# A hand-written instruction list, written anew: chunked state-space scan and squared-ReLU feed-forward on one Trainium2 core

## The chip, the cores and the metric

The kernel runs on one core of a Trainium2 chip. The metric is the device time of one launch in microseconds (us). An execution under the profiler gives a trace, and from it a profile: which engine did what, when, and what released it. The engines are TensorE (PE, its weight loads PEld), VectorE (DVE), ScalarE (ACT), GpSimd (POOL) and SyncE (SP), which here only issues transfers. Each runs its own instructions in order, and they wait for one another by semaphores.

## The reference

A state-space scan over 4 batches, 8 heads and 768 positions in chunks of 32, and on its output a feed-forward layer with a squared ReLU:

```python
cum = np.cumsum(la, axis=-1)                       # la: log of the clipped a
L = np.exp(cum[:, :, :, None] - cum[:, :, None, :]) * causal
M = np.einsum('bhin,bhjn->bhij', Cc, Bc) * L
y[:, :, sl] = M @ xc + (Cc @ state) * np.exp(cum)[..., None]
state = decay_full * state + sum(Bc * xc * decay_from_j)
...
h = np.maximum(x @ w_in, 0.0)                      # x: y as 3072 x 256
return h * h @ w_out                               # w_in 256 x 2048, w_out 2048 x 256
```

Inputs and output are float32.

## The kernel before

**Units.** The work is cut into 12 units (L86): unit k is batch k % 4 and the third k // 4 of the positions, 256 positions of all 8 heads. Unit k's output T[k] is block k of the feed-forward layer. A block has eight steps: a first product, `mm1` (L398, written a0 to a7 for block 0, b0 to b7 for block 1, and so on), a ReLU on ACT into `hb` (L410), a square on DVE (L413, written qa0 and so on), and a second product, `mm2` (L424, A0 to A7). Step 7 of a block ends with its store.

**Preparing a unit.** The running products P of a come from a clamp (`clamp`, ac0 and ac1), a scan on DVE (`scan`, sk0 and sk1) and a small product on TensorE (`prep_p`). ac0, sk0 and `first_p` (sp) make P0 for the first third (units 0 to 3), from the loads fa0 and fa1; ac1, sk1 and `second_p` (p) make the rest, from la0 to la3. C is multiplied by P (`prep_c`, pc), B is copied (`prep_b`, pb), both into the tile jt of the unit; x is multiplied by 1/P (`prep_x`, px). For units 0 to 3 jt is transposed on TensorE (`ph_tr`, tr, with trC and trB for unit 0) and copied out of PSUM (`ph_trc`, tc); from unit 4 on by a DMA of SP. Then come the scores (`ph_mt`, mt, four PSUM banks). A score is masked straight from PSUM by DVE (`ph_mask`, mk) or first copied by ACT (`ph_score`, sc) and then masked by DVE or POOL (`ph_mask_sb`, ms). `ph_u` (u) adds the unit's part to the state, `ph_intra` (ina, inb: two masks each) and `ph_carry` (ca) build the output in two banks, and `ph_t` (t) copies it to T. For the first four units the state goes through `ph_sd_first` (sf, DVE, from PSUM) and `ph_uc` (us, ACT, from PSUM); ph_z and ph_sd (za, zb, sa, sb) carry it on.

**The order.** `ORDER` (L48 to L70) is a list of such tokens, written out by hand. The function `one` (L667) issues them one after the other, and that is the order of each engine's own queue. A letter behind a colon names the engine (v DVE, a ACT, p POOL, s SP); pc, pb and px without one are on POOL. wi0 to wi3 and wo0 to wo3 are the quarters of w_in and w_out, issued by POOL with a cast to bf16 (L137, L142). id12:128 issues 12 products of 128 columns that nobody reads (`idle`, L474). gB3 (`gate`, L130) is a small POOL write to the tile that the load of unit 3's B fills, so this load, and those behind it in SP's queue, wait for POOL.

**Banks.** PSUM has eight banks, and two engines that use one bank are kept apart by semaphores even where they use other columns of it. Banks are given out in turn (`bank`, `pair`, L354 and L360) as the list is read. Unit 0's output is in banks 6 and 7, and its u writes columns 256 to 319 of the same two (L259 to L268). So sf and us read banks that the intra products write.

Of the kernel before, what the change touches and what calls it, by code (L numbers as in the profile page):

```python
# [30 lines left out]
def kernel(  # L31
# [16 lines left out]
    ORDER = """  # L48
        fa1:a jz0:v ef jz1:p id12:128 ti fa0:s la0:s id15:128 pi eb ldB0:s ac0:v ldC0:a sk0 ku sp la1:a pbh0:p hd
        id1:256 pc0:v pbl0:v mb:a id7:128 trC0 ps iv:8:16 tcC0:1:a tcC0:0:v trB0 la2:s tcB0:2:v pk id4:128 iv1:0:8  # L50
        id2:256 ldx0:s mt0 wi0 la3:s px0:v ldC1:s ac1:p su id8:128 ldB1:s wi1 ldx1:s u0:67 mk0 mk0 mk0 pc1:p sc0
        pb1:a tr1 to id5:256 tc1:1:a tc1:0:v jz2:a ms0:p sk1 fq sf0 wo0 wi2 px1:p mt1 ina0 inb0 ca0 mk1 mk1 t0:aa
        sc1 us0 pp1:a mk1 a0 ldC2:s a1 u1 ina1 ms1:v pc2 inb1 p2 sf1 ca1 t1:va us1 a3 qa1 ldB2:s qa0 wo1 wi3 a2
        wo2 b0 qa3 qb0 b1 qb1 fr b2 b3 A0 A1 B0 pb2:p B1 tr2 zb0 qb3 b4 a4 iv:32:64 zb1 tc2:1:v qa2 tc2:0:v b5 sb1
        sb0 qb4 ldx2:s a5 qb2 qa4 mt2 gB3 sc2 ldB3:s ldC3:s B3 iv:16:32 px2 mk2 sc2 A3 ms2:v A2 mk2 qa5 a6 b6
        ms2:p B2 a7 qb5 pb3:a qa6 b7 A5 u2 ina2 ldx3:s inb2 sf2 wo3 pc3 px3 ld4 A4 tr3 ca2 tc3:1:v t2:aa B4 us2 B5
        tc3:0:v u3:45 pc4 mt3 us3 sc3 c5 qb7 qb6 mk3 za3 pb4 ld5 c3 qa7 c4 qc5 c0 tr4 qc3 px4 pb5 sa3 c1 c6 ld6
        qc4 pc5 tr5 qc0 A6 px5 pq A7 wm c2 B6 c7 C0 ms3:v mk3 qc6 mk3 qc7 afC2 pc6 pb6 B7 C3 C6 C4 qc1 bk rg4 C1
        qc2 d1 d0 za4 sa4 mk4 mk4 d3 mk4 C5 d4 qd0 d2 mk4 px6 C2 C7 ld7 zb4 qd1 sb4 qd2 qd3 zb3 rg5 sb3 D0 tr6 mk5
        za5 zb5 sa5 sb5 D1 iv:64:96 mk5 d5 qd4 D2 pb7 d6 qd5 d7 qd6 D3 zb2 e0 qd7 mk5 e1 qe0 sb2 D4 mk5 D5 ld8 pc7  # L60
        e2 qe1 D6 e3 qe2 px7 D7 rg6 e4 qe3 za6 sa6 tr7 zb6 mk6 e5 qe4 sb6 e6 qe5 e7 qe6 mk6 E0 E1 E2 E3 ld9 px8
        mk6 f0 qe7 E4 f1 qf0 pc8 E5 pb8 E6 mk6 f2 qf1 f3 qf2 E7 rg7 mk7 F0 f4 qf3 za7 tr8 F1 F2 f5 qf4 f6 qf5 f7
        qf6 g0 qf7 zb7 sa7 sb7 mk7 F3 mk7 F4 pc9 pb9 px9 ld10 g1 qg0 F5 mk7 g2 qg1 F6 g3 qg2 F7 rg8 za8 zb8 sa8
        sb8 g4 qg3 G0 mk8 tr9 g5 qg4 G1 mk8 g6 qg5 G2 g7 qg6 G3 mk8 h0 qg7 G4 pc10 pb10 px10 ld11 h1 qh0 G5 mk8 h2
        qh1 G6 h3 qh2 G7 rg9 za9 zb9 sa9 sb9 h4 qh3 H0 mk9 tr10 h5 qh4 H1 mk9 h6 qh5 H2 h7 qh6 H3 mk9 i0 qh7 H4
        pc11 pb11 px11 i1 qi0 H5 mk9 i2 qi1 H6 i3 qi2 H7 rg10 za10 zb10 sa10 sb10 i4 qi3 I0 mk10 tr11 i5 qi4 I1
        mk10 i6 qi5 I2 i7 qi6 I3 mk10 j0 qi7 I4 j1 qj0 I5 mk10 j2 qj1 I6 j3 qj2 I7 rg11 za11 zb11 sa11 sb11 j4 qj3
        J0 mk11 j5 qj4 J1 mk11 j6 qj5 J2 j7 qj6 J3 mk11 k0 qj7 J4 k1 qk0 J5 mk11 k2 qk1 J6 k3 qk2 J7 rg12 k4 qk3
        K0 k5 qk4 K1 k6 qk5 K2 k7 qk6 K3 l0 qk7 K4 l1 ql0 K5 l2 ql1 K6 l3 ql2 K7 l4 ql3 L0 l5 ql4 L1 l6 ql5 L2 l7
        ql6 L3 ql7"""  # L70
# [172 lines left out]
    def mm(begun, i, quads, dst, w, v, pos):  # L243
        need = [(i, q) for q in quads if (i, q) not in begun]
        begun.update(need)
        assert len(need) in (0, len(quads))
        nc.tensor.matmul(dst, w, v, start=bool(need), stop=False, skip_group_check=True,  # L247
                         **({} if pos is None else {"tile_position": pos}))
# [92 lines left out]
    def ph_sd_first(k):  # L341

        v, b = live[k], UNITS[k][0]
        S_d = spool.tile([128, 256], BF16, tag=f"Sd{b}0", name=f"Sd{k}_0")
        nc.vector.tensor_tensor(  # L345
            out=_fap(S_d, 0, [[128, 2], [32, 4], [1, 32]]),
            in0=_fap(pp, v["h"][0] * 512 + 256, [[32, 2], [0, 4], [1, 32]]),
            in1=_fap(Pquad, 4 * total(0, b, 0), [[0, 2], [1, 4], [0, 32]]), op=ALU.mult)
# [108 lines left out]

    with tc.manual_schedule():
# [78 lines left out]
        def clamp(m, eng):  # L537
            eng.tensor_scalar(out=a_cl[m], in0=a_nat[m], scalar1=1e-6, scalar2=1.0, op0=ALU.max, op1=ALU.min)  # L538
# [237 lines left out]
```

## Time and profile before

| | |
|---|---|
| runs | 117.34, 117.55, 115.72 us (median 117.34) |
| the profiled execution | 116.09 us |
| its span, first to last instruction | 114.4 us |
| mean granted TensorE clock | 0.985 |
| bytes read from and written to HBM | 10.58 MB, 3.15 MB |

The span is cut into 40 slices in the page; a digit is a share in tenths. A row of a stage has its start and end, its length, busy us and instructions of each engine, and at the end the granted clock, the DMA share and GB/s. A row of the chain has a start, a length, and the engine and line that the end of the program depended on at that time. A row of the timeline has a start, a length, engine, line, operation, what is written and read, and how many; in brackets stands how long the engine had been idle before, and what released it.

### The profile page before, as it was taken

The numbers are of one execution on the slowest core, as the hardware profiler recorded it, in microseconds if no ns is written. First come the engines' busy times: TensorE is split into PE (matmuls) and PEld (weight loads), VectorE is DVE, ScalarE is ACT, GpSimd is POOL, SyncE is SP. The second block draws the span as 40 slices with busy tenths as digits, with TensorE's granted clock in tenths as the row PEclk, the third lists the DMA queues.
The fourth block names the chain that finished last, engine by engine and source line by source line (L and its number), as shares of the span: only waits on it lengthen the run. The fifth ranks groups of instructions, "written<-read, shape, count | busy, mean of one in ns | idle before, by whom it ended". The sixth has DMA issues, their size and how long they took to land.

```text
span 114.4 us, 4062 instructions
## 1 busy us (share of the span) xinstructions
PE 108.4 (95%) x1658; PEld 96.5 (84%) x1658; DVE 84.4 (74%) x185; ACT 77.4 (68%) x158; POOL 52.2 (46%) x98
## 2 busy tenths in 40 slices
PE   7967899999999999999999999999999999999990
PEld 7845499898898889989989989989889899899980
DVE  2697566998899799989965989659578388345430
ACT  1744777677794785686587687786777776966840
POOL 7699950499298946659402769047020020000000
PEclk9999599999999999999999999999999999999999
DMA  2999999099998908988628538350051020020202
GB/s 40 198 196 193 217 196 188 10 183 169 189 163 140 317 10 181 215 192 164 131 80 158 112 113 149 87 145 19 6 141 22 6 95 0 14 83 0 92 6 92
DMA packets 47827, 13.47 MB, mean 118 GB/s; under 512 B 44288, under 2 KB 45888, under 8 KB 47808
## 3 DMA queue, kind: packets, MB, share of 16 engines
q1 hardware_dynamic: 44864, 10.88, 45.9%
q0 software_dynamic: 1664, 2.10, 11.4%
q10 hardware_dynamic: 1280, 0.23, 1.0%
q8 instruction: 13, 0.21, 0.7%
q14 instruction: 6, 0.05, 0.1%
HBM read 10.58 MB, written 3.15 MB: 120 GB/s over the span
## 4 chain that ended last, share of the span: by engine, by line
PE 87%; POOL 3%; DMA 3%; SPq 2%; issue 1%; ACT 1%; DVE 0%; ACTq 0%
PE pp L405 38%; PE pp L432 37%; PE pp L247 7%; PE pp L222 3%; DMA a_nat<-in_a_dram 3%; POOL mts L240 1%; SPq L565 1%; SPq L126 1%; POOL jt L159 1%; POOL w_in_b L140 1%; PE pp L197 1%; ACT T L210 1%; DVE Sd L345 0%; POOL a_cl L538 0%; SPq L116 0%
## 5 line engine op out<-in xcount | busy, mean ns | idle before, releaser
L410 ACT ACTIVATE hb<-pp 128x512 bf16<-128x512 f32 x96 | 54.6, 603 | 22.5 <-PE pp L405 21.4
L416 DVE TENSOR_TENSOR h<-hb 128x512 bf16<-128x512 bf16 x96 | 46.0, 498 | 12.1 <-ACT hb L410 11.8
L405 PE MATMUL pp<-T,w_in_b 128*128 128x256 bf16 x384 | 54.2, 276 | 0.5 <-ACT T L210 0.5
L432 PE MATMUL pp<-w_out_b,h 128*128 128x256 bf16 (+1 forms) x400 | 53.8, 268 | 0.0
L405 PEld LDWEIGHTS <-w_in_b 128*128 128x128 bf16 x384 | 41.8, 114 | 3.1 <-issue 1.8
L432 PEld LDWEIGHTS <-h 128*128 128x128 bf16 x400 | 37.7, 98 | 4.3 <-issue 0.6
L231 DVE TENSOR_TENSOR mts<-pp,mask 128x512 bf16<-128x512 f32 x43 | 28.5, 678 | 0.9 <-PE pp L222 0.9
L333 POOL TENSOR_TENSOR Sd<-z,Pquad 128x256 bf16<-128x256 f32 x16 | 10.6, 666 | 33.9 <-DVE z L317 24.0
L179 POOL TENSOR_TENSOR xs<-x_nat,Pinv 128x256 bf16<-128x256 f32 (+1 forms) x19 | 14.7, 788 | 3.8 <-DMA x_nat<-in_x_dram 2.4
L159 POOL TENSOR_TENSOR jt<-C_nat,P_sb 128x128 bf16<-128x128 f32 x22 | 9.5, 451 | 0.0
L317 DVE SCALAR_TENSOR_TENSOR z<-z,Ptot,us 128x64 f32<-128x64 f32 x8 | 2.4, 296 | 6.6 <-ACT us L301 5.5
L439 ACT COPY osb<-pp 128x512 f32<-128x512 f32 x11 | 6.4, 583 | 0.4 <-PE pp L432 0.4
L247 PE MATMUL pp<-mts,xs 64*32 64x128 bf16 x384 | 6.1, 226 | 0.5 <-DVE Sd L345 0.5
L477 PE MATMUL pp<-const-bfloat16-1.0 128*128 128x128 bf16 (+1 forms) x54 | 5.7, 275 | 0.8 <-PEq L760 0.8
L477 PEld LDWEIGHTS <-const-bfloat16-1.0 128*128 128x128 bf16 x54 | 4.6, 124 | 0.9 <-issue 0.8
L284 ACT CAST T<-pp 128x512 bf16<-128x512 f32 x7 | 4.1, 586 | 1.8 <-PE pp L247 1.5
L247 PEld LDWEIGHTS <-xs 64*32 64x32 bf16 x384 | 4.4, 94 | 0.8 <-issue 0.7
L222 PE MATMUL pp<-bct 32*64 32x256 bf16 x192 | 5.1, 280 | 0.0
L167 POOL CAST jt<-B_nat 128x256 bf16<-128x256 f32 x9 | 4.3, 473 | 1.1 <-DMA B_nat<-in_B_dram 1.1
L247 PE MATMUL pp<-bct,Sd 128*128 128x128 bf16 x40 | 4.3, 223 | 0.0
L210 ACT CAST T<-pp 128x256 bf16<-128x256 f32 x9 | 3.1, 376 | 1.5 <-PE pp L247 1.2
L197 PE MATMUL pp<-eye_b,jt 128*128 128x128 bf16 x24 | 2.5, 221 | 1.2 <-ACT Ptot L531 0.7
(67 smaller groups left out, 57.6 us busy)
## 6 DMA issues: line engine op xcount, KB each, us to landing
x_nat<-in_x_dram SPq DMA_DIRECT2D x12, 256.0 KB, 4.0
out_dram<-osb SPq DMA_DIRECT2D x11, 256.0 KB, 2.2
B_nat<-in_B_dram SPq DMA_DIRECT2D x12, 128.0 KB, 3.2
C_nat<-in_C_dram SPq DMA_DIRECT2D x11, 128.0 KB, 3.3
w_in_b<-in_moe_w_in_dram POOLq DMA_DIRECT2D x4, 256.0 KB, 5.9
w_out_b<-in_moe_w_out_dram POOLq DMA_DIRECT2D x4, 256.0 KB, 5.1
C_nat<-in_C_dram ACTq DMA_DIRECT2D x1, 128.0 KB, 2.5
bct<-jt SPq DMA_TRANSPOSE x8, 2.9
```

The costliest lines, as they stand in the source:

```text
L159: eng.tensor_tensor(out=_fap(jt[k % 3], 128 + 144 * g, [[384, 2], [32, 4], [1, 16]]), in0=_fap(loaded[k]["C"], 128 * g, [[16, 2], [32, 4], ...
L179: eng.tensor_tensor(out=_fap(xs, 256 * r, [[256, 2 // n], [32, 8], [1, 32]]), in0=_fap(loaded[k]["x"], 32 * r, [[32, 2 // n], [64, 8], [1, ...
L222: nc.tensor.matmul(pp[64 * u:64 * u + 64, q, r * 256:r * 256 + 256], bct[32 * q:32 * q + 32, r, 0, u * 64:u * 64 + 64], _fap(bct[32 * q:32 ...
L231: nc.vector.tensor_tensor(out=live[k]["mts"][:, q].rearrange("p r g i -> p (r g i)"), in0=pp[:, q, :], in1=mask, op=ALU.mult)
L247: nc.tensor.matmul(dst, w, v, start=bool(need), stop=False, skip_group_check=True, **({} if pos is None else {"tile_position": pos}))
L333: nc.gpsimd.tensor_tensor(out=_fap(S_d, 0, [[128, 2], [32, 4], [1, 32]]), in0=_fap(z, 0, [[32, 2], [0, 4], [1, 32]]), in1=_fap(Pquad, 4 * ...
L405: nc.tensor.matmul(pp[:, h, i * 256:(i + 1) * 256], _fap(w, g * w.shape[2] + (o // 2) * 512 + 2 * (o % 2) + i, [[4, 128]]), T[blk][:, g].r ...
L410: nc.scalar.activation(out=hb.rearrange("p i t -> p (i t)"), in_=pp[:, h, :], func=AF.Relu)
L416: nc.vector.tensor_tensor(out=h2, in0=hb, in1=hb, op=ALU.mult)
L432: nc.tensor.matmul(dst, h2[:, i, r * 128:(r + 1) * 128], w_out_b[gi][:, 2 * o + i, c0:c1], start=first, stop=(fp == 7 and i == 1), skip_gr ...
L439: nc.scalar.copy(out=osb, in_=pp[:, 6 if blk == 1 else 7, :])
L477: nc.tensor.matmul(pp[:, h, 0:int(cols)], ones_b[:, 0:128], ones_b[:, 0:int(cols)] if dep is None else dep, start=True, stop=True, skip_gr ...
```

## The change

The list is written anew up to the token tr6; from there on it is the same. In words, by engine, up to unit 2:

- **SP** loads a's pieces in another order: fa0, la3, B0, la0, x0, la2 instead of fa0, la0, B0, la2, x0, la3. x0 stays the fifth load.
- **POOL**: ac1 is gone. wi0 stands behind jz1 and ahead of the cast of B0 (pbl0), wi1 right behind that cast, ahead of pc1 and ms0. px1 follows wi2, then wo1, pc2 and sb0. wi3, wo2, sb1, pq and gB3 follow; wi3 and wo2 stand behind tr2 in the list. pb2 leaves POOL for DVE.
- **DVE**: mb comes first, hd ahead of sk0, then jz0, iv1, pc0, iv, ac1 and sk1 ahead of px0. tc1:1 stays, tc0's copies go to ACT. Unit 2 has three direct masks (mk2) instead of two.
- **ACT**: jz2 ahead of ps, the three copies of unit 0's transposes, t1 with both halves.
- **PE**: ina0 and inb0 ahead of mt1 and of the product with sf0's result; the idle products at other places.

Two pieces of code are new. `u1:4` puts the first half of unit 1's u into bank 4, at column 256, so that `sf1` reads a bank that the intra products don't write; `us1` then takes two copies. And `second_p` only issues its products; the two copies out of PSUM are a token of their own, `pd`, which stands ahead of t1.

The diff, the list up to unit 3's masks:

```diff
-        fa1:a jz0:v ef jz1:p id12:128 ti fa0:s la0:s id15:128 pi eb ldB0:s ac0:v ldC0:a sk0 ku sp la1:a pbh0:p hd
-        id1:256 pc0:v pbl0:v mb:a id7:128 trC0 ps iv:8:16 tcC0:1:a tcC0:0:v trB0 la2:s tcB0:2:v pk id4:128 iv1:0:8
-        id2:256 ldx0:s mt0 wi0 la3:s px0:v ldC1:s ac1:p su id8:128 ldB1:s wi1 ldx1:s u0:67 mk0 mk0 mk0 pc1:p sc0
-        pb1:a tr1 to id5:256 tc1:1:a tc1:0:v jz2:a ms0:p sk1 fq sf0 wo0 wi2 px1:p mt1 ina0 inb0 ca0 mk1 mk1 t0:aa
-        sc1 us0 pp1:a mk1 a0 ldC2:s a1 u1 ina1 ms1:v pc2 inb1 p2 sf1 ca1 t1:va us1 a3 qa1 ldB2:s qa0 wo1 wi3 a2
-        wo2 b0 qa3 qb0 b1 qb1 fr b2 b3 A0 A1 B0 pb2:p B1 tr2 zb0 qb3 b4 a4 iv:32:64 zb1 tc2:1:v qa2 tc2:0:v b5 sb1
-        sb0 qb4 ldx2:s a5 qb2 qa4 mt2 gB3 sc2 ldB3:s ldC3:s B3 iv:16:32 px2 mk2 sc2 A3 ms2:v A2 mk2 qa5 a6 b6
-        ms2:p B2 a7 qb5 pb3:a qa6 b7 A5 u2 ina2 ldx3:s inb2 sf2 wo3 pc3 px3 ld4 A4 tr3 ca2 tc3:1:v t2:aa B4 us2 B5
-        tc3:0:v u3:45 pc4 mt3 us3 sc3 c5 qb7 qb6 mk3 za3 pb4 ld5 c3 qa7 c4 qc5 c0 tr4 qc3 px4 pb5 sa3 c1 c6 ld6
+        eb fa0:s fa1:a ti ldC0:a mb:v ef ac0:v la3:s pi id9:128 ldB0:s id3:256 id8:128 la1:a la0:s hd sk0 id2:128
+        sp ldx0:s jz2:a jz0:v id9:128 la2:s iv1:0:8 pc0:v ps iv:8:16 trC0 ku pbh0:a ac1:v tcC0:0:a jz1:p id2:128
+        sk1 wi0 pbl0:p ldC1:s trB0 px0:v id5:128 tcC0:1:a ldB1:s tcB0:2:a id1:128 mt0 u0:67 mk0 mk0 mk0 wi1
+        id2:128 pk sc0 ldx1:s pb1:a su pc1:p id8:128 to tr1 ina0 ms0:p tc1:0:a fq inb0 ldC2:s pp1:a tc1:1:v sf0
+        ldB2:s wo0 mt1 ca0 t0:aa mk1 mk1 id1:256 wi2 mk1 sc1 px1:p ms1:v a1 a0 wo1 u1:4 p2 ina1 sf1 us0 inb1 ca1
+        pd2 t1:aa us1 a2 qa0 a3 ldx2:s zb0 qa2 b0 b1 pc2 qa1 qb0 b2 qb1 fr b3 qa3 pb2:v iv:32:64 iv:16:32 qb2 zb1
+        A0 sb0 A1 B0 B1 tr2 wi3 tc2:1:a b5 qb3 tc2:0:v b4 a4 a5 mt2 A2 B2 B3 A3 wo2 sb1 pq gB3 mk2 mk2 mk2 sc2
+        ldB3:s px2 qa5 qa4 qb5 ldC3:s qb4 a6 pb3:a a7 b7 ms2:p b6 wo3 u2 ina2 ldx3:s inb2 A4 B5 pc3 sf2 ca2 tr3
+        t2:vv A5 tc3:1:a tc3:0:v us2 ld4 qa7 B4 px3 qb6 u3:45 pc4 mt3 us3 sc3 c2 c0 wm mk3 qa6 ld5 pb4 qb7 tr4 za3
...
-    def ph_u(k, h, begun):
+    def ph_u(k, h, begun, own=False):
         v, last = live[k], UNITS[k][1] == 2
         v["h"] = h
+        v["uat"] = [(4, 128 * (k + 1)) if own and i == 0 else (h[i], 256) for i in range(2)]
...
-                    mm(begun, i, [q], pp[32 * q:32 * q + 32, h[i], 256:320],
+                    at, c = v["uat"][i]
+                    mm(set() if r == 0 and own and i == 0 else {(0, q)} if own and i == 0 else begun, i, [q], pp[32 * q:32 * q + 32, at, c:c + 64],
...
             nc.tensor.matmul(pp[:, h, 128:144], spread, pick_p[1], start=True, stop=True, skip_group_check=True)
+            busy.add(h)
+            second["h"] = h
+
+        second = {}
+
+        def second_out():
+            h = second["h"]
+            busy.discard(h)
             A.copy(out=Ptot[:, 8:24], in_=pp[:, h, 128:144])
             A.copy(out=P_sb[:, :, 32:96], in_=_fap(pp, h * 512, [[64, 2], [1, 64]]))
...
-            v["h"] = tuple(int(c) for c in hs) if hs else pair()
+            own = hs == "4"
+            v["h"] = ((6, 7) if k == 0 else pair()) if own else tuple(int(c) for c in hs) if hs else pair()
```

More of the change, by code (lines that the diff above doesn't have):

```diff
@@ L54 @@
-        wo2 b0 qa3 qb0 b1 qb1 fr b2 b3 A0 A1 B0 pb2:p B1 tr2 zb0 qb3 b4 a4 iv:32:64 zb1 tc2:1:v qa2 tc2:0:v b5 sb1
-        sb0 qb4 ldx2:s a5 qb2 qa4 mt2 gB3 sc2 ldB3:s ldC3:s B3 iv:16:32 px2 mk2 sc2 A3 ms2:v A2 mk2 qa5 a6 b6
-        ms2:p B2 a7 qb5 pb3:a qa6 b7 A5 u2 ina2 ldx3:s inb2 sf2 wo3 pc3 px3 ld4 A4 tr3 ca2 tc3:1:v t2:aa B4 us2 B5
-        tc3:0:v u3:45 pc4 mt3 us3 sc3 c5 qb7 qb6 mk3 za3 pb4 ld5 c3 qa7 c4 qc5 c0 tr4 qc3 px4 pb5 sa3 c1 c6 ld6
-        qc4 pc5 tr5 qc0 A6 px5 pq A7 wm c2 B6 c7 C0 ms3:v mk3 qc6 mk3 qc7 afC2 pc6 pb6 B7 C3 C6 C4 qc1 bk rg4 C1
@@ L59 @@
[L59 to L68, printed above, removed]
@@ L69 @@
-        K0 k5 qk4 K1 k6 qk5 K2 k7 qk6 K3 l0 qk7 K4 l1 ql0 K5 l2 ql1 K6 l3 ql2 K7 l4 ql3 L0 l5 ql4 L1 l6 ql5 L2 l7
-        ql6 L3 ql7"""
+        eb fa0:s fa1:a ti ldC0:a mb:v ef ac0:v la3:s pi id9:128 ldB0:s id3:256 id8:128 la1:a la0:s hd sk0 id2:128
+        sp ldx0:s jz2:a jz0:v id9:128 la2:s iv1:0:8 pc0:v ps iv:8:16 trC0 ku pbh0:a ac1:v tcC0:0:a jz1:p id2:128
+        sk1 wi0 pbl0:p ldC1:s trB0 px0:v id5:128 tcC0:1:a ldB1:s tcB0:2:a id1:128 mt0 u0:67 mk0 mk0 mk0 wi1
+        id2:128 pk sc0 ldx1:s pb1:a su pc1:p id8:128 to tr1 ina0 ms0:p tc1:0:a fq inb0 ldC2:s pp1:a tc1:1:v sf0
@@ new lines @@
+        qc2 c5 ld6 qc0 sa3 px4 c3 c4 pc5 pb5 tr5 c6 qc3 B6 qc6 A6 A7 c7 c1 ms3:v zb3 mk3 mk3 C0 C3 C2 C6 B7 bk rg4
+        qc4 qc5 qc1 C4 qc7 za4 mk4 mk4 mk4 mk4 sb3 d4 C1 d0 d1 d2 C5 px5 sa4 C7 pc6 qd0 qd2 zb4 qd1 afC2 ld7 d3
+        px6 rg5 qd3 sb4 D0 pb6 tr6 mk5 za5 zb5 sa5 sb5 D1 iv:64:96 mk5 d5 qd4 D2 pb7 d6 qd5 d7 qd6 D3 zb2 e0 qd7
+        mk5 e1 qe0 sb2 D4 mk5 D5 ld8 pc7 e2 qe1 D6 e3 qe2 px7 D7 rg6 e4 qe3 za6 sa6 tr7 zb6 mk6 e5 qe4 sb6 e6 qe5
+        e7 qe6 mk6 E0 E1 E2 E3 ld9 px8 mk6 f0 qe7 E4 f1 qf0 pc8 E5 pb8 E6 mk6 f2 qf1 f3 qf2 E7 rg7 mk7 F0 f4 qf3
@@ new lines @@
+        za7 tr8 F1 F2 f5 qf4 f6 qf5 f7 qf6 g0 qf7 zb7 sa7 sb7 mk7 F3 mk7 F4 pc9 pb9 px9 ld10 g1 qg0 F5 mk7 g2 qg1
+        F6 g3 qg2 F7 rg8 za8 zb8 sa8 sb8 g4 qg3 G0 mk8 tr9 g5 qg4 G1 mk8 g6 qg5 G2 g7 qg6 G3 mk8 h0 qg7 G4 pc10
+        pb10 px10 ld11 h1 qh0 G5 mk8 h2 qh1 G6 h3 qh2 G7 rg9 za9 zb9 sa9 sb9 h4 qh3 H0 mk9 tr10 h5 qh4 H1 mk9 h6
+        qh5 H2 h7 qh6 H3 mk9 i0 qh7 H4 pc11 pb11 px11 i1 qi0 H5 mk9 i2 qi1 H6 i3 qi2 H7 rg10 za10 zb10 sa10 sb10
+        i4 qi3 I0 mk10 tr11 i5 qi4 I1 mk10 i6 qi5 I2 i7 qi6 I3 mk10 j0 qi7 I4 j1 qj0 I5 mk10 j2 qj1 I6 j3 qj2 I7
@@ L71 @@
+        rg11 za11 zb11 sa11 sb11 j4 qj3 J0 mk11 j5 qj4 J1 mk11 j6 qj5 J2 j7 qj6 J3 mk11 k0 qj7 J4 k1 qk0 J5 mk11
+        k2 qk1 J6 k3 qk2 J7 rg12 k4 qk3 K0 k5 qk4 K1 k6 qk5 K2 k7 qk6 K3 l0 qk7 K4 l1 ql0 K5 l2 ql1 K6 l3 ql2 K7
+        l4 ql3 L0 l5 ql4 L1 l6 ql5 L2 l7 ql6 L3 ql7"""
     WIN = [(0, 2), (2, 4), (4, 6), (6, 8)]
@@ L295, in ph_uc @@
         us = spool.tile([128, 2, 64], FP32, tag="us", name=f"us{k}", bufs=8)
-        h = v["h"]
-        if h[1] == h[0] + 1 and not last:
-            nc.scalar.copy(out=us, in_=_fap(pp, h[0] * 512 + 256, [[512, 2], [1, 64]]))
+        at = [512 * h + c for h, c in v["uat"]]
+        if not last and (at[1] - at[0] == 512 or v["uat"][0][0] == 4 and v["uat"][0][1] != 256):
+            nc.scalar.copy(out=us, in_=_fap(pp, at[0], [[at[1] - at[0], 2], [1, 64]]))
         else:
             for i in range(2 - last):
-                nc.scalar.copy(out=us[:, i], in_=pp[:, h[i], 256:320])
+                nc.scalar.copy(out=us[:, i], in_=_fap(pp, at[i], [[1, 64]]))
         v["us"] = us
@@ L346, in ph_sd_first @@
             out=_fap(S_d, 0, [[128, 2], [32, 4], [1, 32]]),
-            in0=_fap(pp, v["h"][0] * 512 + 256, [[32, 2], [0, 4], [1, 32]]),
+            in0=_fap(pp, v["uat"][0][0] * 512 + v["uat"][0][1], [[32, 2], [0, 4], [1, 32]]),
             in1=_fap(Pquad, 4 * total(0, b, 0), [[0, 2], [1, 4], [0, 32]]), op=ALU.mult)
@@ L630, in first_u @@
             v["begun"] = set()
-            ph_u(k, v["h"], v["begun"])
+            ph_u(k, v["h"], v["begun"], own)
         def intra(k, part):
@@ L698, in one @@
                 "mb": lambda: causal(eng), "pk": picked, "ac": lambda: clamp(k, eng), "sk": lambda: scan(k), "sp": first_p, "pp": lambda: second_pick(eng),
-                "su": first_sums, "to": first_total, "fq": first_quad, "p": lambda: second_p(), "pq": second_quad,
+                "su": first_sums, "to": first_total, "fq": first_quad, "p": lambda: second_p(), "pd": second_out, "pq": second_quad,
                 "ps": lambda: A.copy(out=P_sb[:, :, 0:32], in_=P0.rearrange("p (r c) -> p r c", r=2)),
```

## The prediction

> **What bounds the kernel now.** I read the page first (busy times and slices), then the stages with the granted clock, then the chain of work in order of time. Two lines of the page:
>
> ```profile
> PE 108.4 (95%) x1658; PEld 96.5 (84%) x1658; DVE 84.4 (74%) x185; ACT 77.4 (68%) x158; POOL 52.2 (46%) x98
> PEclk9999599999999999999999999999999999999999
> ```
>
> TensorE fills 95% of the span, and the one slice with a low granted clock is the fifth (11.4 to 14.3 us). So the end can move only by what TensorE wastes: waits, idle products, half clock. The stages that follow are cut where the clock changes; the columns are busy us and count per engine, then clock, DMA share, GB/s.
>
> ```profile
> 4.10:7.51 3.41, 3.28 (x70) 2.40 (x66) 2.86 (x10) 1.74 (x6) 2.49 (x5) 1.00 1.00 193
> 7.51:10.92 3.41, 1.88 (x31) 1.20 (x35) 2.62 (x6) 1.68 (x4) 3.38 (x6) 1.00 1.21 201
> 10.92:14.33 3.41, 2.94 (x62) 1.82 (x66) 2.22 (x4) 2.18 (x7) 3.40 (x7) 0.50 1.17 211
> ```
>
> The clock is halved for exactly one stretch of 3.41 us, just behind a stretch in which TensorE was busy for only 1.88 us. The chain shows what the prologue waited for, and where the dense part begins:
>
> ```profile
> 3.26 2.92 DMA a_nat<-in_a_dram
> 6.27 0.41 POOL a_cl L538
> 7.37 0.73 POOL w_in_b L140
> 8.18 0.77 POOL jt L159 x2
> 8.94 1.10 POOL mts L240
> 10.05 0.33 POOL Pquad L534
> 10.40 0.43 DVE Sd L345
> 10.88 0.79 PE pp L247 x31
> 11.67 0.64 ACT T L210 x2
> 12.35 1.87 PE pp L405 x8
> 14.22 0.60 PE pp L247 x42
> 15.66 2.66 PE pp L405 x24
> ```
>
> The late part of a lands at 3.26 + 2.92 = 6.18 us. Then GpSimd is the bottleneck to 10.4: clamp, an issue of w_in, unit 1's C (pc1), the fourth mask (ms0), Pquad. Then come Sd, the intra products, T0, and a0/a1 at 12.35: 8 products in 1.87 us, 0.234 each, against 2.66 / 24 = 0.111 each from 15.66 on. From 14.2 on TensorE hardly stops. The question is therefore when the new list reaches a0/a1 and when its dense part begins, against 12.35 and 15.66 here.
>
> **The change, part by part.** From tr6 on the two lists agree, and the products with work in them are the same, so I work out the start of the dense part only.
>
> *DVE chain to the masks.* ac1 goes from GpSimd to DVE, and sk1 is moved ahead of px0. DVE is in order, so px0 and the first masks now wait for the late a, whose last piece is still the sixth load of SP: 6.18 us again. Prices:
>
> ```profile
> 5.32 0.37 ACT L210 COPY bct<-pp 128x256 bf16<-128x256 bf16 x1
> 6.46 0.59 ACT L236 CAST sc<-pp 128x512 bf16<-128x512 f32 x1 [0.38 <-PE pp L222]
> 2.61 0.22 DVE L538 TENSOR_SCALAR a_cl<-a_nat 64x128 f32<-64x128 f32 x1 [1.29 <-DMA a_nat<-in_a_dram]
> 6.12 0.69 DVE L179 TENSOR_TENSOR xs<-x_nat,Pinv 128x512 bf16<-128x512 f32 x1
> 6.73 1.88 DVE L231 TENSOR_TENSOR mts<-pp,mask 128x512 bf16<-128x512 f32 x3
> 9.61 0.73 DVE L470 TENSOR_TENSOR_SCAN cp<-a_cl,const-float32-0.0 128x128 f32<-128x128 f32 x1
> 12.82 0.52 DVE L240 TENSOR_TENSOR mts<-sc,mask 128x512 bf16<-128x512 bf16 x1 [0.20 <-ACT sc L236]
> ```
>
> The clamp has 64 rows here and 128 after, with the same 128 elements a row; I take 0.22. (On GpSimd the chain has 0.41 in it.) 6.20 + 0.22 + 0.73 + 0.69 + 1.88 = 9.72 for the third mask; it was at 6.73 + 1.88 = 8.61. So this edit costs the masks 1.1 us. What it buys: GpSimd no longer clamps, and ms0, which ended at 8.94 + 1.10 = 10.04, needs only C of unit 1 and the copied score. The transposed B and C of unit 0 are now copied by ACT alone, behind ps at 5.3: pbh0 and three copies of up to 0.37 with some overlap end near 6.5, so mt0 goes at 6.6 (it was 5.9); the score (0.59) follows at 7.15, is there by 7.75, and ms0 ends near 8.9. Both stay ahead of the masks. mb on DVE (no such row; I bound it by 0.2, the clamp, and 0.6, just over the mask product of as many bf16 at 0.52, and take 0.4) runs from 2.35 and costs nothing, because DVE has 0.4 us of slack before 6.2.
>
> *Banks and T0.* sf0 reads unit 0's bank. It used to stand before the intra products, and the chain goes through it to them; now ina0 and inb0 stand first. inb0 goes at 9.8 and ends near 10.2; sf0 (0.42) at 10.25 to 10.67; the carry at 10.75, ending at 11.1; both T copies by 11.5. a1 starts at 11.6, which is **0.75 us earlier** than 12.35. Unit 1 gets the same by its own bank (u1:4): sf1 no longer waits for the intra products. Its us1 falls into two copies on ACT, 0.2 to 0.3 us, which delay only hb. p2's bank is kept until pd2; ACT reads it before t1, and five banks still serve, so I put that at 0 (up to 0.3 if b0 has to wait).
>
> *The clock.* The idle products now, narrow and wide:
>
> ```profile
> L477 PE MATMUL pp<-const-bfloat16-1.0 128*128 128x128 bf16 x46 | 4.7, 275 | 0.8 <-PEq L760 0.8
> L477 PE MATMUL pp<-const-bfloat16-1.0 128*128 128x256 bf16 x8 | 1.4, 275 | 0.0
> ```
>
> The new list has 46 narrow and 4 wide ones, at other places; none stands on the chain but the first 22, which end at 3.5 (27 of them ended at 3.8 before), ahead of cp at 3.8. Between 7.51 and 10.92 TensorE would do u0, 10 idle products, the sums, tr1, ina0, inb0, mt1 and the start of the carry: about 2.6 us by the rows' spans, against 1.88 that was followed by half clock, and 2.94 and 3.28 that were followed by full clock. 2.6 is nearer to 2.94, so I take full clock: a1 and a0 last 8 x 0.109 = 0.87 instead of 1.87 and end at 12.5.
>
> The Trainium skill's "TensorE: Matmul & The Clock Gate" (Part 1) has the clock fall only after an idle window of about 3.4 us, and (Part 4) transposes not counted as busy. The stretch of 3.41 us agrees; that 1.88 us of work still led to half clock does not agree with an idle window. By that rule the new list stays warm, which would give the sum below; by the row of 1.88 alone it is open.
>
> *Loads.* This edit speaks against the change. GpSimd's first six preparations are the same work and end at 4.19, but wi0 then follows at 4.2 (it was at 5.26, behind pbh0), and wi1 at about 5.45 (it was at 7.37). The rows are of short stretches: issues in 5.0:5.3 with us to landing, the queues in 7.6:7.7, 8:9 and 9.5:10.25 with packets and MB (q0 is the weights' queue, q1 SP's).
>
> ```profile
> x_nat<-in_x_dram SPq DMA_DIRECT2D x1, 256.0 KB, 5.2
> w_in_b<-in_moe_w_in_dram POOLq DMA_DIRECT2D x1, 256.0 KB, 5.5
> q0 software_dynamic: 3, 0.00, 22.3%
> q0 software_dynamic: 161, 0.16, 99.2%
> q1 hardware_dynamic: 98, 0.02, 15.2%
> q1 hardware_dynamic: 1008, 0.13, 110.5%
> 4.00 0.19 POOL L481 TENSOR_SCALAR_AFFINE_SELECT quad<-quad 128x4 f32<-128x4 f32 x1
> 5.26 0.93 POOL L140 DMA_DIRECT2D w_in_b<-in_moe_w_in_dram  x1 [0.26 <-issue]
> 7.37 0.78 POOL L140 DMA_DIRECT2D w_in_b<-in_moe_w_in_dram  x1
> 11.63 1.07 POOL L179 TENSOR_TENSOR xs<-x_nat,Pinv 128x512 bf16<-128x512 f32 x1
> ```
>
> While a weight quarter moves it takes 0.16 of 0.18 MB; without one, SP's queue moves 0.13 MB in 0.75 us. x of unit 1 landed at 5.04 + 5.2 = 10.2 with one quarter ahead of its end. Now two quarters stand ahead: 0.26 MB more at 0.18 MB/us is +1.4, so 11.7. px1 can't go at 10.6, when GpSimd is free, but at 11.8, and ends at 11.8 + 1.07 = 12.9. TensorE is through with a0 at 12.5 and stops 0.45 us before u1. C and B of unit 1 are nearly in when the quarter begins to move (its first packets were at 7.6, some 2.4 us behind the issue at 5.26: now 6.6) and have 0.4 us of slack. Second and third weights (wo0, wi2) go 1 us earlier, wi3 and wo2 about as before, since GpSimd waits for no transposition in between, only for zb0 and zb1. They are needed 2 us or more after they land. SP's next loads hang on gB3, whose wait is this row of SP's waits:
>
> ```profile
> SPq L126 <- POOL B_nat L135: 11.2, 1, 11.2
> ```
>
> gB3 follows sb1 and Pquad on GpSimd, at about 20 instead of 21.8. The later loads keep their distance to TensorE: 0.
>
> *From u1 to the dense part.* In the chain u1, the intra products, p2 and the carry run from 14.22 to 15.66: 1.44 us, nearly all at full clock. 12.95 + 1.44 = 14.4, against 15.66: **1.27 us earlier**. T1 is now copied by ACT alone, in 0.65 us instead of on two engines, and is ready at 15.3, when a2 and a3 (14.4 + 0.87) have just ended: 0.1 us lost.
>
> *Behind that.* The stages from 15 to 20 and from 40 to 50 us:
>
> ```profile
> 15.00:20.00 5.00, 5.00 (x54) 4.70 (x51) 3.59 (x10) 3.74 (x10) 0.83 (x2) 1.00 1.15 193
> 40.00:50.00 10.00, 10.00 (x196) 9.04 (x194) 9.96 (x23) 7.01 (x14) 6.37 (x11) 1.00 0.70 142
> ```
>
> DVE gets a third direct mask in unit 2 (0.6 in place of the copied one's 0.47), t2 and pb2, and loses t1 and half of tc2 and tc3: +0.2 us. It was free for 1.4 us between 15 and 20, so I put that at 0 (up to 0.5 if u3, whose banks wait for t2 on DVE and us2 on ACT, stops TensorE).
>
> **Sum.** 1.27 - 0.1 = 1.15 us earlier. The profiled execution took 116.09 (span 114.4 and 1.7 around it), so 114.9. The runs shown have a median of 117.34, which is 1.25 above the profiled execution, and two of three lie there; the trace can't show why. Carried over whole this would give 116.2, and not at all 114.9. I put the forecast in the middle, **115.5 us**; this likeliest case alone reaches from 114.4 to 116.8.
>
> **The rivals.**
>
> *The clock falls all the same.* If 2.6 us is not enough, or the stretches of 3.41 us lie elsewhere, a0 and a1 last 1.87 again: 11.65 + 1.87 = 13.5. Then px1 is covered, but p2 and the intra products are at half clock until 14.3 (+0.5): dense part at 15.4, gain 0.2 to 0.5. Time 115.7 by the profile, 116.3 with half the distance to the median. For it: the 1.88 us row. Against: the fuller stretch. The skill's page (Part 1) also calls the window free-running; by that the half clock could fall on any stretch in any run, before and after. One trace shows one position.
>
> *x of unit 1 stays behind all early weights (the slower side).* wo0 is issued near 9.3 and moves from about 11.7. If x1 still lacks a piece then, it gets 0.02 of 0.18 MB until wo0 and wi2 have passed (0.51 MB, 2.8 us): landing at 15.3, u1 at 16.4, dense part at 17.9, which is 2.2 us later than now: 118.3 by the profile, 118.9 with the half distance. It decides from a landing of x1 past 13.0 on: from there px1 ends later than u1's 14.15 of now. Against it: my sum has x1's last bytes moved about 0.7 us before wo0 starts. A landing between 12 and 13 takes the gain step by step to nothing, 116.1 to 116.7.
>
> *The gain is given back later.* DVE is busy for 9.96 us of the 10 from 40 to 50. If it can't run ahead with TensorE, squares come late there, and the end stays within 0.3 us of now: 116.1 to 117. Against it: the same instructions lie there in both lists, and DVE's waits before 40 us are for ACT and TensorE, which both come earlier.
>
> **How the numbers follow.** Likeliest case (full clock, x1 near 11.7): 0.45. Half clock again: 0.22. x1 between 12 and 13, or given back: 0.18. x1 behind wo0 and wi2, or another stop of that size: 0.15. The range takes 114.3 (nothing of the distance to the median, and x1 early, which saves the 0.45 us stop) to 117.8 (half way into the last case): about 0.8. 2%, which is about what a measurement of this kernel can tell from no change, is 2.35 us: faster means under 115.0, slower over 119.7. A good half of the likeliest case and a little of the second lie under 115.0: 0.30. Only the upper part of the last case lies over 119.7: 0.10. Within 2%: 0.60.
>
> **What would show it.** In the changed profile: third mask ending near 9.7 and a1 near 11.6 (chain through DVE's scan and px0 instead of GpSimd's clamp); granted clock 1.0 in the slices from 11 to 14 us and 0.11 us for each of the first eight products; GpSimd's px1 waiting for x_nat until 11.7 or so; TensorE's dense part from 14.4; gB3 near 20. Wrong would be: a chain that runs through a DMA of x or B of unit 1 past 13 us, a half clock over a0 and a1, or TensorE waits of over 0.5 us between 20 and 50 us.

## The result and the profile after

The changed kernel is slower. On the same chip it took 119.04 us (median; 118.31 to 119.86) against 117.08 us (115.72 to 117.55) for the kernel before: a ratio of 1.031, interval 1.024 to 1.038. Here and below a ratio is taken over fast runs alone, so it is not that of the two medians (1.017 here). The forecast was 115.5 us. The profiled execution took 118.46 us (span 116.8), against 116.09 (span 114.4).

Two lines of the page of the changed kernel, busy time and granted clock by slices:

```profile
PE 108.7 (93%) x1654; PEld 96.2 (82%) x1654; DVE 82.6 (71%) x184; ACT 77.8 (67%) x161; POOL 50.6 (43%) x96
PEclk9997559999999999999999999999999999999998
```

TensorE has as much to do as before (108.7 against 108.4 us busy), but its share fell from 95 to 93%, and the low clock now covers two slices and part of a third. The chain of work in order of time (start, length, what) shows what the prologue waits for now:

```profile
4.39 6.53 DMA B_nat<-in_B_dram
10.94 0.02 ACTq L167
11.00 0.41 ACT jt L167
11.47 0.80 PE pp L197 x6
12.28 0.73 PE pp L247 x26
13.06 0.44 DVE Sd L347
13.97 0.38 ACT T L210
14.40 1.87 PE pp L407 x8
17.48 0.60 PE pp L247 x28
18.08 2.62 PE pp L407 x24
```

The chain no longer goes through GpSimd. It goes through the load of unit 1's B, which is under way for 6.53 us; behind it come ACT's cast of it (pb1), the transposition tr1, the intra products, T0, and a0 and a1 at 14.40, where the kernel before had 12.35. The dense part begins at 18.08 instead of 15.66. These 2.42 us are the whole difference of the spans (116.8 - 114.4 = 2.4): from the start of the dense part to the end there are 98.7 us in both.

The two rows of the waits that belong to it (total, times, longest):

```profile
ACT jt L167 <- DMA B_nat<-in_B_dram: 3.5, 1, 3.5
PEld L197 <- ACT jt L167: 2.5, 1, 2.5
```

The loads issued between 4.2 and 4.6 us, with the us from issue to landing, first before, then after:

```profile
C_nat<-in_C_dram SPq DMA_DIRECT2D x1, 128.0 KB, 2.8
B_nat<-in_B_dram SPq DMA_DIRECT2D x1, 128.0 KB, 3.2
```

```profile
w_in_b<-in_moe_w_in_dram POOLq DMA_DIRECT2D x1, 256.0 KB, 6.0
C_nat<-in_C_dram SPq DMA_DIRECT2D x1, 128.0 KB, 4.4
B_nat<-in_B_dram SPq DMA_DIRECT2D x1, 128.0 KB, 6.5
```

B of unit 1 is issued at the same time as before and takes twice as long. What moved meanwhile stands in the queues' rows of 7 to 9 us of the changed kernel (packets, MB, share of the 16 engines; q0 carries the weights, q1 SP's loads):

```profile
q0 software_dynamic: 226, 0.22, 78.8%
q1 hardware_dynamic: 457, 0.07, 27.8%
```

The first quarter of w_in, which the new list issues at 4.33, takes 0.22 of the 0.29 MB of these 2 us. SP's queue has twice as many packets, but they are small: 0.07 MB / 457 is 0.15 KB each, against 0.22 MB / 226 = 1 KB. The Trainium skill's "DMA: Bandwidth & Descriptors" (Queues, rings and completion order) says that a DMA engine takes turns between its queues by packets. The rows agree in part: the counts are not equal (226 and 457), but the larger packets get the larger share of the bytes, whichever load was asked for first.

The stages, cut where the clock changes (busy us and count of PE, PEld, DVE, ACT, POOL; clock; DMA share; GB/s):

```profile
6.90:10.32 3.42, 1.36 (x28) 1.01 (x27) 2.62 (x5) 0.58 (x1) 1.80 (x3) 1.00 1.03 150
10.32:13.73 3.41, 2.19 (x56) 1.35 (x57) 1.01 (x3) 1.36 (x5) 1.80 (x5) 0.50 1.23 191
13.73:17.14 3.41, 3.16 (x36) 1.90 (x34) 2.66 (x6) 2.38 (x6) 2.30 (x4) 0.50 1.12 189
```

The wait for B leaves TensorE busy for 1.36 us of a stretch; the clock is halved behind it, and stays so for a second stretch. In the kernel before it was one stretch.

So there is a theory: the first quarter holds B of unit 1 back, and the half clock follows from the wait. The rivals: that another part of the change (the masks behind DVE's scan, the bank of its own, the order of the products) costs the time, with B's landing only happening beside it; that the second quarter does it; that the clock falls by itself.

### The profile page after: what moved, and what is told of

It reads as the page before. It is cut to its first block, busy times and chain, and to the rows that moved or that the text cites. A ratio compares the mean times of both kernels' runs of the same rounds, so it can differ in the third digit from the quotient of the medians.

```text
span 116.8 us, 4053 instructions
## 1 busy us (share of the span) xinstructions
PE 108.7 (93%) x1654; PEld 96.2 (82%) x1654; DVE 82.6 (71%) x184; ACT 77.8 (67%) x161; POOL 50.6 (43%) x96
## 3 DMA queue, kind: packets, MB, share of 16 engines
q0 software_dynamic: 1664, 2.10, 11.7%
## 4 chain that ended last, share of the span: by engine, by line
PE 87%; DMA 6%; SPq 3%; ACT 1%; issue 1%; DVE 0%; ACTq 0%; DVEq 0%
PE pp L407 38%; PE pp L434 36%; PE pp L247 8%; DMA B_nat<-in_B_dram 6%; PE pp L222 3%; SPq L575 1%; PE pp L197 1%; SPq L126 1%; PE pp L456 1%; DVE Sd L347 0%; SPq L116 0%; ACT jt L167 0%; ACT T L210 0%; PE pp L551 0%; ACT us L300 0%
## 5 line engine op out<-in xcount | busy, mean ns | idle before, releaser
L418 DVE TENSOR_TENSOR h<-hb 128x512 bf16<-128x512 bf16 x96 | 45.2, 492 | 12.8 <-ACT hb L412 12.4
L231 DVE TENSOR_TENSOR mts<-pp,mask 128x512 bf16<-128x512 f32 x44 | 29.0, 681 | 2.8 <-PE pp L222 2.8
L335 POOL TENSOR_TENSOR Sd<-z,Pquad 128x256 bf16<-128x256 f32 x16 | 10.7, 667 | 35.4 <-DVE z L319 25.8
L179 POOL TENSOR_TENSOR xs<-x_nat,Pinv 128x256 bf16<-128x256 f32 (+1 forms) x19 | 14.6, 787 | 0.9 <-DMA x_nat<-in_x_dram 0.8
L167 POOL CAST jt<-B_nat 128x256 bf16<-128x256 f32 x8 | 3.8, 481 | 3.2 <-PE pp L407 1.9
L197 PEld LDWEIGHTS <-jt 128*128 128x128 bf16 x24 | 1.7, 108 | 3.0 <-ACT jt L167 2.5
```

Source lines behind the costliest of these rows:

```text
L179: eng.tensor_tensor(out=_fap(xs, 256 * r, [[256, 2 // n], [32, 8], [1, 32]]), in0=_fap(loaded[k]["x"], 32 * r, [[32, 2 // n], [64, 8], [1, ...
L231: nc.vector.tensor_tensor(out=live[k]["mts"][:, q].rearrange("p r g i -> p (r g i)"), in0=pp[:, q, :], in1=mask, op=ALU.mult)
L335: nc.gpsimd.tensor_tensor(out=_fap(S_d, 0, [[128, 2], [32, 4], [1, 32]]), in0=_fap(z, 0, [[32, 2], [0, 4], [1, 32]]), in1=_fap(Pquad, 4 * ...
L418: nc.vector.tensor_tensor(out=h2, in0=hb, in1=hb, op=ALU.mult)
```

## The experiments

The kernels ran in three groups, each with the kernel before on its chip. Its median was 115.23 us beside the first four, 115.28 beside the next four, and 116.12 beside the last three. Ratios are against that kernel on the same chip. In the diffs, three dots within a line stand for tokens left out.

**Both quarters later** (the changed kernel; wi0 goes behind the cast of B0, wi1 behind ms0)

```diff
-        sk1 wi0 pbl0:p ldC1:s ... mk0 mk0 mk0 wi1
+        sk1 pbl0:p wi0 ldC1:s ... mk0 mk0 mk0
-        ... tr1 ina0 ms0:p tc1:0:a ...
+        ... tr1 ina0 ms0:p wi1 tc1:0:a ...
```

> The changed list, but the first w_in quarter is issued behind the cast of B0 (near 5.0 us) and the second behind ms0 (near 9). Theory (the early weights take the transfer engines from B of unit 1): B1 lands by 7.8 instead of 10.9, tr1 starts near 9.0 instead of 11.5, a1 near 11.4 instead of 14.4, the dense part near 14.2 instead of 18.1; time 114.5 to 116. Rival (the price is the masks, 1 us later by ac1 and sk1 ahead of px0): the masks still end at 9.5, and the time stays at 118.3 or more. Rival (the idle products of the new list are too few, whatever B1 does): a1 near 11.4 but half clock over a1 and a0, dense part near 16, time 116.5 to 117.5.

Measured: 115.39 us, ratio 1.002 (0.999 to 1.006). B of unit 1, issued at 4.37, landed 3.1 us later, at 7.5. Its chain, and the stage behind which the clock could have fallen:

```profile
5.14 6.47 DMA x_nat<-in_x_dram
11.76 1.05 POOL xs L179
12.85 0.25 PE pp L247 x16
14.43 2.81 PE pp L407 x24
```

```profile
10.09:13.51 3.42, 2.16 (x44) 1.67 (x36) 3.13 (x6) 2.45 (x6) 3.14 (x6) 1.00 1.12 161
```

Two tokens moved undo the whole loss, with all else of the change left in. a1 starts at 11.51, x of unit 1 lands at 11.62, px1 (L179) follows, and the dense part begins at 14.43.

**That part alone, in the kernel before** (wi0 ahead of pbh0, wi1 behind it; nothing else)

```diff
-        ... sp la1:a pbh0:p hd
+        ... sp la1:a wi0 pbh0:p wi1 hd
-        id2:256 ldx0:s mt0 wi0 la3:s ... ldB1:s wi1 ldx1:s
+        id2:256 ldx0:s mt0 la3:s ... ldB1:s ldx1:s
```

> The list before, with only the first two w_in quarters issued early: ahead of the cast of B0 and right behind it. Theory: B1 lands near 10.9 instead of 7.5, tr1 waits for it, a0 starts near 14.3 instead of 12.35, dense part near 17.5; time 118.5 to 119.5. Rival (the loss is in the order of the DVE and TensorE work): GpSimd is even freed of an issue between ac1 and pc1, and the time is that of before or up to 0.5 us less.

Measured: 120.24 us, ratio 1.042 (1.036 to 1.048). Its chain:

```profile
4.36 6.23 DMA B_nat<-in_B_dram
11.09 0.49 PE pp L197 x6
14.52 1.87 PE pp L405 x8
```

The early issue alone makes the kernel before as slow as the changed one: the same load, the same 1.87 us at half clock. With the first experiment this shows the cause from both sides.

**Only the second quarter later**

```diff
-        ... mk0 mk0 mk0 wi1
+        ... mk0 mk0 mk0
-        ... tr1 ina0 ms0:p tc1:0:a ...
+        ... tr1 ina0 ms0:p wi1 tc1:0:a ...
```

> The changed list, with only the second w_in quarter moved behind ms0; the first stays at 4.3 us. Theory: one quarter (0.26 MB at 0.16 MB/us, moving from 6.7 to 8.3) stands ahead of B1 instead of two: B1 lands near 9, tr1 near 9.7, dense part 15 to 16, time 115.5 to 117. If the first quarter alone is enough to hold B1 back to 10.9: 119. If only the second one does: as with both moved, 114.5 to 116.

Measured: 118.18 us (116.67 to 118.69 in four runs, at mean clocks of 0.985 to 0.956), ratio 1.018 (1.010 to 1.026), more than was expected. The profiled run took 118.51 us at 0.971. Its chain and two of its stages:

```profile
4.38 5.56 DMA B_nat<-in_B_dram
12.78 1.87 PE pp L407 x8
16.98 1.71 PE pp L407 x8
```

```profile
9.00:12.41 3.41, 1.70 (x57) 0.99 (x57) 1.56 (x4) 1.55 (x6) 2.83 (x6) 1.00 0.99 156
12.41:15.83 3.42, 3.07 (x35) 2.14 (x34) 2.60 (x7) 2.16 (x5) 2.30 (x4) 0.50 1.12 200
```

The first quarter alone holds B to 9.94. Changed lists with both quarters early had it at 10.92 (the changed kernel), 10.08 (the same again) and 9.90 (with filled wait, below), so the second quarter adds between nothing and one us. I had expected that the clock would hold with so much less of a wait; it did not, after 1.70 us of work in a stretch, nor in any of the other three runs.

**The wait filled with idle products** (the changed kernel, 48 narrow idle products ahead of tr1 instead of 8)

```diff
-        ... pc1:p id8:128 to tr1 ina0 ...
+        ... pc1:p id48:128 to tr1 ina0 ...
```

> The changed list with 48 instead of 8 narrow idle products ahead of tr1, which fill the wait for B1 (2.3 us at 0.057 us each). B1 still lands at 10.9 and a1 stays at 14.4. If half clock is a price of its own on top of the wait: the clock stays at 1.0, a1 and a0 take 0.87 instead of 1.87 and what follows them 1.4 instead of 1.8, dense part near 16.5, time 117.0 to 117.7. If the half clock is hidden behind px1 and the loads: u1 waits for px1 until 14.6 or later, and the time falls by 0.5 us at most.

Measured: 116.39 us, ratio 1.011 (1.008 to 1.015), mean clock 1.000. Its chain:

```profile
8.36 2.93 PE pp L479 x48
11.29 0.33 PE pp L197 x6
13.42 1.06 PE pp L407 x8
15.98 2.62 PE pp L407 x24
```

The weights are as early as in the changed kernel and B lands late (9.90). The 48 products run to 11.29, about 0.8 us longer than tr1 would have had to wait (in the changed kernel it starts 0.55 us behind B's landing). So tr1 starts at nearly the same time as in the changed kernel, 11.29 against 11.47. Yet a0 and a1 take 1.06 us instead of 1.87, and the dense part begins 2.1 us sooner (15.98 against 18.08): some 1.9 of these 2.1 us, all but what tr1 is earlier, go with the half clock. The other 1.55 us, down to the first experiment's 14.43, go with the wait itself, the products' excess included. By the ratios the two parts are 2.3 us (1.031 - 1.011, from two chips) and 1.0 us (1.011 - 1.002).

**The kernel before, filled** (it had one half-clock stretch in its profile; idle products ahead of tr1, ina0 and a0)

```diff
-        pb1:a tr1 to ... px1:p mt1 ina0 ...
-        sc1 us0 pp1:a mk1 a0 ...
+        pb1:a id18:128 tr1 to ... px1:p mt1 id8:128 ina0 ...
+        sc1 us0 pp1:a mk1 id7:128 a0 ...
```

> The list before, with narrow idle products in the waits of TensorE between 7.4 and 12.4 us: 18 ahead of tr1, 8 ahead of ina0, 7 ahead of a0. Theory (half clock follows from TensorE's own idle time, and it alone spreads the times of the list before between 114.6 and 117.5): every run at a clock of 0.996 or more, all times between 114.6 and 115.6, the median at that of the undisturbed runs of before. Rival (half clock falls on any stretch, whatever TensorE does): runs with clocks of 0.97 to 0.985 and 116.8 to 117.5 us stay as frequent. If filling costs time itself, up to 0.3 us more.

Measured: 115.28 us (114.91 to 115.59 in 12 runs, all at a mean clock of 1.00), ratio 1.001 (0.999 to 1.003). The kernel before beside it had the same median, and spread from 114.75 to 118.0 us in 29 runs; its runs over 116 us but one are at a mean clock of 0.97 to 0.985. So the spread of the kernel before, and the 1.25 us between the median shown and the profiled run that I could not explain, fit half-clock stretches that it meets in some runs; with TensorE kept busy there were none in 12 runs. The clocks of the three runs shown ahead of the prediction are not on record.

**x of unit 1 ahead of the first quarter** (the first experiment, with GpSimd waiting for x of unit 0 before wi0, and px1 ahead of wo0)

```diff
-        sk1 pbl0:p wi0 ldC1:s ...
+        sk1 pbl0:p afx0 wi0 ldC1:s ...
-        ldB2:s wo0 mt1 ... sc1 px1:p ms1:v a1 ...
+        ldB2:s px1:p wo0 mt1 ... sc1 ms1:v a1 ...
```

> As the changed list with the weights late, but the first w_in quarter waits for x of unit 0 on GpSimd (a copy of one column ahead of it), so it moves from about 8.6 instead of 7.5, and px1 stands ahead of wo0 and wi2. Theory (x of unit 1, landing at 11.6 behind the first quarter, is what keeps the dense part at 14.4 there): x1 lands near 9.5, px1 runs near 10.3, u1 follows a0 without a wait at 12.4, dense part between 13.8 and 14.2 (the second quarter must be in for a2), time 0.3 to 0.6 us under that list. Rival: the first quarter lands past 11.5 and a1 waits for it instead, or DVE's masks of unit 1 (to 13.1) hold the intra products: no gain, 115.2 to 115.6.

Measured: 118.55 us (116.72 to 118.88 in six runs), ratio 1.019 (1.011 to 1.027): more than even the rival allowed. The profiled run took 118.81 us. Its chain, and its two stages at half clock:

```profile
6.61 6.08 DMA w_in_b<-in_moe_w_in_dram
12.73 1.41 PE pp L407 x8
16.46 2.23 PE pp L407 x10
```

```profile
13.31:16.72 3.41, 3.41 (x67) 2.27 (x65) 1.04 (x4) 2.15 (x7) 2.20 (x5) 0.50 1.11 172
16.72:20.14 3.42, 3.42 (x18) 2.43 (x16) 1.11 (x3) 2.34 (x7) 0.73 (x2) 0.50 0.90 137
```

x of unit 1 landed at 9.5 and px1 began at 10.72, 1 us sooner than in the first experiment, but now a1 waits for its weights. Much of the time goes with the half clock behind that wait: the two runs at mean clocks of 1.0 and 0.983 took 116.93 and 116.72 us, the other four, at 0.971 to 0.956, 118.43 us or more. Each of the two loads is late when the other goes first; the first experiment stands between them.

**The masks ahead of the scan** (the first experiment, ac1 and sk1 behind the three direct masks)

```diff
-        ... pbh0:a ac1:v tcC0:0:a jz1:p id2:128
-        sk1 pbl0:p wi0 ... mk0 mk0 mk0
+        ... pbh0:a tcC0:0:a jz1:p id2:128
+        pbl0:p wi0 ... mk0 mk0 mk0 ac1:v sk1
```

> As the changed list with the weights late, but ac1 and sk1 stand behind the three masks of unit 0 on DVE, as sk1 did before. Prices by the rows: the masks end near 8.6 instead of 9.3. If the order on DVE costs what it delays: a1 0.7 us earlier. If it is covered (sf0 needs Pquad, which GpSimd makes behind ms0 and the second quarter's issue at 10.0 to 10.25): sf0 stays at 10.3, a1 at 11.5, and the time within 0.3 us of that list.

Measured: 115.10 us, ratio 0.998 (0.995 to 1.001). Two rows of its chain:

```profile
11.10 1.09 POOL xs L179
14.12 2.81 PE pp L407 x24
```

The masks end at 8.74 instead of 9.33, a1 starts at 11.11, and the dense part 0.3 us sooner. In these two traces the scan ahead of the masks costs that much and no more, since what sets sf0 is Pquad on GpSimd (9.60 to 9.85) and behind it px1; the intervals of the two ratios overlap.

**Without the bank of its own** (the first experiment, with `u1` in its pair and pd2 right behind p2)

```diff
-        ... a1 a0 wo1 u1:4 p2 ina1 ...
-        pd2 t1:aa ...
+        ... a1 a0 wo1 u1 p2 pd2 ina1 ...
+        t1:aa ...
```

> As the changed list with the weights late, but unit 1's u in its own region's banks and the two copies of p2 right behind it, as before. If the bank of its own saves a wait: sf1 has to stand clear of the intra products of bank h0, ina1 and inb1 wait for sf1 or it for them, and the dense part begins 0.3 to 0.6 us later, 115.6 to 116.0. If it makes no difference: 115.2 to 115.5.

Measured: 115.54 us, ratio 1.004 (1.001 to 1.006). Two rows of its chain:

```profile
13.96 0.44 DVE Sd L347
15.06 2.62 PE pp L407 x24
```

sf1 now stands on the chain between the intra products, and the dense part begins 0.6 us later than with the own bank (14.43). In the trace that part of the change does what the prediction gave it. The times don't show it: 1.004 here and 1.002 there, on different chips, with intervals that overlap, and the place of pd2 moved with it.

**A version meant to be best** (the masks ahead of the scan; besides, wi1 between pc1 and ms0, px1 ahead of wo0, idle products ahead of ca0 and a1)

```diff
-        ... pc1:p id8:128 to tr1 ina0 ms0:p wi1 ... sf0
-        ldB2:s wo0 mt1 ca0 t0:aa mk1 mk1 id1:256 wi2 mk1 sc1 px1:p ms1:v a1 a0
+        ... pc1:p wi1 id8:128 to tr1 ina0 ms0:p ... sf0
+        ldB2:s px1:p wo0 mt1 id6:128 ca0 t0:aa mk1 mk1 wi2 mk1 sc1 ms1:v id9:128 a1 a0
```

> The list with the weights late and the masks first, and more: the second w_in quarter issued behind pc1 instead of behind ms0, px1 ahead of wo0 and wi2, narrow idle products ahead of the carry (6) and of a1 (9). Theory: there a2 waited 0.3 us for the second quarter (landed 14.07) and u1 came at 12.2; now the second quarter lands near 13, px1 starts when x1 lands (10.7), sf0 stays near 10.0, dense part near 13.6 instead of 14.1: 0.3 to 0.6 us under that list and under the list before, 114.5 to 115.0, clock 1.0 in every run. Rival: x1 lands later behind the second quarter, or ms0, 0.75 later, holds inb0 and sf0: no gain, 115.1 to 115.5.

Measured: 115.34 us, ratio 1.000 (0.996 to 1.005): no gain. Unit 1's clamp in its timeline, and GpSimd's fourth mask; then the same clamp in the version with the masks ahead of the scan alone:

```profile
8.97 1.21 DVE L540 TENSOR_SCALAR a_cl<-a_nat 128x128 f32<-128x128 f32 x1
8.93 1.16 POOL L240 TENSOR_TENSOR mts<-sc,mask 128x512 bf16<-128x512 bf16 x1
```

```profile
8.65 0.29 DVE L540 TENSOR_SCALAR a_cl<-a_nat 128x128 f32<-128x128 f32 x1
```

wi1 moved GpSimd's mask to the time of DVE's clamp, and the clamp lasts to 10.18, just behind the mask's end at 10.09. Without wi1 ahead of it the mask had ended at 8.86, and the clamp took 0.29; with nothing on GpSimd it takes 0.23 (6.46 to 6.69 in the changed kernel). sf0 follows 0.9 us later and a1 1.3 us (12.40 against 11.11); part of the rest is the added idle products, which end at 11.83 ahead of the carry, though sf0 had ended at 11.22. px1 gained nothing by its new place: x of unit 1 landed later (at 11.0 against 10.7), as the rival had it, and px1 began at 11.11, against 11.10.

**B of unit 1 ahead of x of unit 0** (the changed kernel, one load moved)

```diff
-        sp ldx0:s jz2:a ... tcC0:1:a ldB1:s tcB0:2:a
+        sp ldB1:s ldx0:s jz2:a ... tcC0:1:a tcB0:2:a
```

> The changed list with its early weights, but B of unit 1 is loaded ahead of x of unit 0 in SP's queue. Theory (a load that still moves at 6.7 us, when the first quarter begins, is held back; nothing is special to B): B1 lands near 5.5, x0 and the last piece of a 0.7 later, and C1 is now the load that moves at 6.7: it lands at 9 to 10 instead of 8.4, pc1 and tr1 follow at 10 to 10.8, and the time is 0 to 1.5 us under the changed list, well over before. Rival (it is B1's own cast, or its place behind the copied score on ACT): tr1 near 9.5, time 115.5 to 116.5.

Measured: 119.8 us, ratio 1.034 (1.026 to 1.043). Two rows of its chain:

```profile
4.53 5.95 DMA C_nat<-in_C_dram
14.65 1.87 PE pp L407 x8
```

B of unit 1, issued at 2.82, landed at 5.82, and C of unit 1 took its place: it landed at 10.48, GpSimd's pc1 waited 4.4 us for it, and tr1 came at 11.47 as in the changed kernel. So it is not something about B: here the other small load that was still on the queue when the quarter moved is held.

**The changed kernel once more, unaltered**

> The changed list once more, unaltered, beside the two others on their chip. As recorded before: B1 landing near 10.9, a1 near 14.4, clock under 0.975, 118.3 to 119.9 us.

Measured: 119.4 us (median of four, 116.77 to 120.95), against 116.12 for the kernel before. B was under way for 5.65 us and landed at 10.08; the chain has the same steps. That is 0.8 us sooner than in the first trace, and a1 began at 13.36, 1 us sooner. Yet this execution took 120.19 us, since the half clock lasted for three stretches (10.89 to 21.13) instead of two.

## Why the prediction was wrong

**The step that failed** stands under *Loads*: "C and B of unit 1 are nearly in when the quarter begins to move [...] and have 0.4 us of slack". The quarter's issue did move to 4.33, as said. But B and C were not nearly in: B landed at 10.92 instead of 7.55, C at 8.3 instead of 6.7. SP's queue had moved 0.64 MB by 7.0 us, when the weights had 0.02 MB, and its loads up to B make 0.72 MB (four pieces of a at 16 KB, B and x of unit 0, C and B of unit 1). So at least 0.08 MB was still to come (an estimate from these sizes; the trace does not count by load), and in the next 2 us the queue got 0.07 MB, x of unit 1 included. I had quoted the row that tells it, 0.02 MB for SP's queue in a us in which the weights move 0.16 MB, and applied it to x of unit 1 alone. The rival "x of unit 1 stays behind all early weights" was the right mechanism at the wrong load: it was B, which tr1 and everything behind it hang on, and the first two quarters, not wo0 and wi2. x itself landed at 13.3 in the changed kernel, not at 11.7, but px1 ended at 14.5, ahead of the end of a0 at 16.3, so that cost nothing there.

**The clock.** The forecast of full clock rested on 2.6 us of work in the stretch before; tr1 and the intra products were part of it, and both moved behind B. So this step failed by the one before. It was also the larger part: about 2 us of the dense part's start against 1.55 for the wait (2.3 and 1.0 by the ratios). With the quarters late the clock held, as forecast, though after 2.16 us of work, not 2.6.

**What held.** With only the two quarters put later, the rest of the working came out: a1 at 11.51 (11.6 predicted), x of unit 1 landed at 11.62 (11.7), px1 from 11.76 to 12.81 (11.8 to 12.9), the dense part from 14.43 (14.4), gB3 at 20.32 (20). The profiled run took 114.98 us, where the sum gave 114.9. That the median of 115.39 meets the forecast of 115.5 is luck, because the half distance in it had no reason. x met its number partly for another reason, since only one quarter was ahead of it there. The third mask ended at 9.52 in the changed kernel (9.7). Behind the dense part's start nothing changed (98.7 us in both): 0 was right.

**Sizes that were off.** The scan was put at 0.73 by the row of the kernel before; in the lists with the new order it took 0.42 to 0.45. The row of 0.73 began beside GpSimd's ms0. In the kernel before, filled, the two lie the same way and the scan takes 0.73 again; in the kernel before with the weights early, ms0 ends at 11.44, the scan starts at 11.80 and takes 0.41:

```profile
9.68 0.73 DVE L470 TENSOR_TENSOR_SCAN cp<-a_cl,const-float32-0.0 128x128 f32<-128x128 f32 x1
11.80 0.41 DVE L470 TENSOR_TENSOR_SCAN cp<-a_cl,const-float32-0.0 128x128 f32<-128x128 f32 x1
```

So the price was that of a scan beside the mask, and the new order did not have it there. mb on DVE took 0.29 (0.4 predicted). The masks' 1.1 us of cost were about 0.6 (9.33 against 8.74), and worth 0.3 us at the dense part.

**The distance to the median.** I carried half of 1.25 us over without a reason. The filled kernel before shows what it most likely is: half-clock stretches in some runs. The profiled run of the kernel before had one. At full clock throughout it takes 115.3 us, and against that the change with late quarters gains nothing by the median (1.002), although its profiled run starts the dense part at 14.43, against 15.07 in the filled kernel before. Why these 0.6 us do not show in the median stays open: some of its runs at a clock of 0.996 to 1.0 took 116.1, 116.3 and 117.85 us, and they have no trace.
